# Attention and two feed-forwards: block products in the second feed-forward only, narrow buffers during attention

## The chip, the core and the metric

The kernel runs on one core of one Trainium2 chip. The core has a matrix engine (TensorE, PE in the profile), a vector engine (VectorE, DVE), a scalar engine (ScalarE, ACT), a general engine (GpSimd, POOL) and queues for transfers (DMA, here issued by SyncE, SP). Each engine works through its own instructions in the order in which the program lists them, and waits by semaphores for the others. The metric is the device time of one execution in microseconds; of several executions the median counts.

## What is computed

The reference is a local attention with summaries of blocks, and two feed-forwards behind it. Cut to what matters:

```python
# q, k, v: 2 x 8 x 768 x 64, fp32; moe_w_in 512 x 2048, moe_w_out 2048 x 512, both twice
k_sum, v_sum = blocks of 32 keys: max of k, mean of v
scores = softmax over (keys within 16 positions, 24 block summaries)
x = (scores @ [v, v_sum]) laid out as 1536 tokens x 512
h = x @ w_in;  x = (h * cos(h)) @ w_out            # first feed-forward
h = x @ w_in2; out = (h * clip(h + 3, 0, 6) / 6) @ w_out2   # second
```

All operands are fp32. The kernel keeps that accuracy with a pair for each number, a part in the type fp32r and the rest (`hi` and `lo`), and each product of two matrices becomes three on PE: hi with hi, lo with hi, hi with lo.

## The kernel before

**Stages.** Attention runs in 12 units of 128 tokens (`front(u)`: scores, largest, exponentials `es` with their sums, scaling by `rs` in line 610; `back(u)`: transposes to `pts` in line 625, the weighted sum in line 640, then `xhi` and `xlo`, the tokens for the feed-forwards). The 1536 tokens form three blocks of 512.

**Steps.** A feed-forward's 2048 hidden columns are 16 slices of 128. A step `s` of the list `plan` is one slice for one block: a first product `h` (`mm1`, line 780, twelve matmuls), a `middle`, and a second product (`mm2`, line 874, twelve matmuls) which adds into four banks of PSUM. The middle of the first feed-forward is five operations: a rounding on ACT (line 819), a difference on DVE (821), the sine on ACT (823), a product with `h` (825), then the pair of the result, `ghi` (389) and `glo` (834). Slices come in groups of four, each group for all three blocks in turn. The first 16 steps (`NEARLY`) are halves of 256 columns for blocks 0 and 1 and run during attention; steps 16 to 19 are block 2. Steps 20 to 55 are the rest of the first feed-forward, 56 to 103 the second.

**Sets.** From step `SETS` on (20), the first products of two neighbouring slices are made together (`mm1_set`, line 731): the 2 x 2 blocks of weights and tokens are combined so that seven block products of 256 columns do for eight, 7 x 3 x 2 = 42 matmuls instead of 24 of 512 columns. For that the weights of the two slices are combined and split into `phi` and `plo` (`convert_pair`, two such buffers), the tokens into `txhi` and `txlo` (`tees`; for the first feed-forward `first_tees`, line 705, which needs the sum of `xhi` and `xlo` first), and the products are joined into `hs` in SBUF by two copies (line 389) and five additions on DVE (line 744) per set. Before the sets, a slice's plain weights `whi` and `wlo` for the first product lie in the same memory as `phi` and `plo`, four slices of them.

**Weights.** Each 128 x 512 piece arrives as raw words (`raw`, 32 for each of the two sides, two buffers) and takes five operations to become fp32 values (`nearest`, lines 447 to 466) and two to become a pair (`split`, lines 389 and 406).

**Order.** Nothing stands in the order of the code. `Graph` collects all operations with what they read and write, and `forward` lists them for each engine: the operation that can start first goes first, and among those that can start about then the one with the earliest due time. An operation that may run on DVE or elsewhere is kept off DVE if the other engine would end no later than DVE plus `PATIENCE`; where DVE is still a choice, `UNWANTED` is added to its due time. An activation that needs another function table has `SWITCH` added. Where the planner leaves PE idle, `fill` puts matmuls with zeros into the order (lines 844 and 849), which keep PE working and change nothing. The second product of a step comes `LAG` = 2 steps behind its first.

**Memory.** `ch_c` (the middle's working buffer), `ghi` and `glo` are three buffers each of 512 columns, and a fourth pair once attention's memory is free. That is the operation `switch`: it gives attention's pool back and opens the pool `late`; what needs it reads the key `room`.

## Time and profile before

| | |
|---|---|
| device time, median of 3 runs | 615.45 us (614.9 to 615.78) |
| the profiled execution | 615.68 us |
| its span, first to last instruction | 614.0 us |
| PE busy | 592.5 us, 97% |
| DVE busy | 515.4 us, 84% |
| ACT busy | 389.2 us, 63% |
| POOL busy | 230.4 us, 38% |
| moved by DMA | 51.57 MB, 16 engines busy 25.2% of the span for it |
| granted PE clock, mean | 0.996 |

Times in the profile count from the first instruction. A matmul's row shows when it starts and for how long it is in the engine; as matmuls overlap, the distance between the starts of two of them is the time that one costs. L731 is line 731 of the kernel. `bank_c`, `bank_d` and so on are PSUM banks, their numbers left out.

### The profile page before, as it was taken

How to read it: one execution, taken by the hardware profiler on the slowest of the kernel's cores; microseconds unless marked ns; L12 is line 12 of the kernel's file. 1: busy time of each engine (PE TensorE's matmuls, PEld its weight loads, DVE VectorE, ACT ScalarE, POOL GpSimd, SP SyncE). 2: the span in 40 equal slices, each digit the busy share in tenths (PEclk: the TensorE clock that was granted, in tenths of full speed). 3: DMA queues.
4: the chain of work that ended last, by engine and by line, in shares of the span. 5: the costliest groups of instructions: out<-in, count | busy, mean ns of one | idle time of the engine just before them, and what ended most of it. 6: DMA issues, size and time to landing. Idle time of an engine off the chain costs nothing.

```text
span 614.0 us, 11095 instructions
## 1 busy us (share of the span) xinstructions
PE 592.5 (97%) x4244; PEld 519.5 (85%) x4244; DVE 515.4 (84%) x916; ACT 389.2 (63%) x828; POOL 230.4 (38%) x216
## 2 busy tenths in 40 slices
PE   9989899998998999999989999999999999999997
PEld 6678698887897888988978888999898989889895
DVE  4889997699999999899999999989869984984644
ACT  4889997675667667657776675685845643462321
POOL 5245531444232743473455554434334311520110
PEclk9999999999999999999999999999999999999999
DMA  8768631012112222111212012122312320200111
GB/s 275 226 233 254 183 122 52 2 69 69 34 36 69 69 69 69 70 68 70 76 62 70 25 46 69 49 90 98 108 69 70 114 92 1 70 1 1 69 70 68
DMA packets 17141, 51.57 MB, mean 84 GB/s; under 512 B 2112, under 2 KB 2112, under 8 KB 17088
## 3 DMA queue, kind: packets, MB, share of 16 engines
q1 hardware_dynamic: 17088, 50.86, 25.2%
q8 instruction: 33, 0.54, 0.4%
q14 instruction: 20, 0.16, 0.1%
HBM read 47.71 MB, written 3.15 MB: 83 GB/s over the span
## 4 chain that ended last, share of the span: by engine, by line
PE 55%; DVE 17%; ACT 6%; issue 3%; POOL 2%; DVEq 0%; ACTq 0%; POOLq 0%
PE bank_a L874 15%; PE bank_d L731 12%; PE bank_b L874 7%; PE bank_c L874 7%; PE bank_e L731 6%; PE bank_c L731 6%; DVE ch_c L821 2%; DVE hs L744 2%; DVE glo L834 1%; DVE ch_c L825 1%; DVE cv_t L464 1%; DVE ch_c L830 1%; ACT ch_c L823 1%; POOL cv_y L466 1%; ACT ch_c L819 1%
## 5 line engine op out<-in xcount | busy, mean ns | idle before, releaser
L466 POOL TENSOR_TENSOR cv_y<-cv_t,cv_y 128x512 int32<-128x512 int32 x29 | 42.4, 1463 | 75.9 <-DVE cv_t L464 64.8
L744 DVE TENSOR_TENSOR hs<-bank_d,hs 128x256 f32<-128x256 f32 x108 | 45.1, 421 | 29.3 <-PE bank_d L731 27.2
L834 POOL TENSOR_TENSOR glo<-ch_c,ghi 128x512 fp32r<-128x512 f32 (+1 forms) x28 | 34.2, 1227 | 52.5 <-ACT ghi L389 47.2
L389 ACT CAST ghi<-ch_c 128x512 fp32r<-128x512 f32 (+1 forms) x74 | 43.5, 592 | 11.6 <-DVE ch_c L825 5.4
L828 ACT ACTIVATE ch_c<-hs,three 128x512 f32<-128x512 f32 x48 | 33.7, 722 | 26.8 <-DVE hs L744 26.3
L464 DVE SCALAR_TENSOR_TENSOR cv_t<-raw,cv_t 128x512 int32<-128x512 int32 x64 | 49.2, 780 | 0.2
L457 ACT ACTIVATE cv_t<-raw 128x512 f32<-128x512 f32 x59 | 39.3, 670 | 6.2 <-DMA raw<-in_w_out_dram 2.3
L823 ACT ACTIVATE ch_c<-ch_c,half_pi 128x512 f32<-128x512 f32 (+1 forms) x56 | 35.8, 659 | 8.4 <-DVE ch_c L821 8.3
L830 DVE SCALAR_TENSOR_TENSOR ch_c<-ch_c,hs 128x512 f32<-128x512 f32 x48 | 36.9, 778 | 4.1 <-ACT ch_c L828 2.6
L447 ACT ACTIVATE cv_y<-raw 128x512 int32<-128x512 uint32 x54 | 35.8, 671 | 4.4 <-DVE wlj_out L406 3.5
L834 DVE TENSOR_TENSOR glo<-ch_c,ghi 128x512 fp32r<-128x512 f32 (+1 forms) x54 | 37.0, 692 | 1.7 <-POOL ghi L389 0.7
L731 PE MATMUL bank_d<-xhi,phi 128*128 128x256 f32 x170 | 34.7, 286 | 3.3 <-DVE hs L744 2.4
L731 PEld LDWEIGHTS bank_d<-xhi,phi 128*128 128x128 f32 x170 | 28.4, 189 | 8.3 <-DVE hs L744 3.9
L834 POOL TENSOR_TENSOR glj<-ch_c,ghj 128x512 fp32r<-128x512 f32 x11 | 15.9, 1443 | 51.5 <-ACT ghj L389 48.4
L462 DVE TENSOR_SCALAR cv_t<-cv_t 128x512 int32<-128x512 int32 x64 | 32.5, 516 | 2.3 <-ACT cv_t L457 2.2
L731 PE MATMUL bank_d<-xlo,phi 128*128 128x256 f32 x170 | 34.2, 283 | 0.0
L406 POOL TENSOR_TENSOR plo<-cv_y,phi 128x512 fp32r<-128x512 f32 (+1 forms) x16 | 18.6, 1161 | 41.6 <-DVE phi L389 33.8
L731 PE MATMUL bank_d<-xhi,plo 128*128 128x256 f32 x170 | 34.2, 282 | 0.0
L819 ACT ACTIVATE ch_c<-hs,quarter 128x512 int32<-128x512 f32 x36 | 24.9, 720 | 13.2 <-DVE hs L744 13.1
L821 DVE SCALAR_TENSOR_TENSOR ch_c<-hs,ch_c 128x512 f32<-128x512 f32 x36 | 31.2, 889 | 0.8 <-ACT ch_c L819 0.5
L825 POOL TENSOR_TENSOR ch_c<-hs,ch_c 128x512 f32<-128x512 f32 x14 | 20.7, 1486 | 29.5 <-ACT ch_c L823 29.5
L389 ACT COPY hs<-bank_d 128x256 f32<-128x256 f32 x39 | 14.5, 372 | 26.9 <-PE bank_d L731 26.5
(359 smaller groups left out, 2023.5 us busy)
## 6 DMA issues: line engine op xcount, KB each, us to landing
raw<-in_w_in_dram SPq DMA_DIRECT2D x32, 512.0 KB, 3.5
raw<-in_w_out_dram SPq DMA_DIRECT2D x32, 512.0 KB, 3.4
vcat<-in_vw_dram SPq DMA_DIRECT2D x12, 384.0 KB, 4.3
ktile<-in_kt_dram SPq DMA_DIRECT2D x8, 384.0 KB, 4.4
qt<-in_q_dram SPq DMA_DIRECT2D x12, 256.0 KB, 5.4
total<-in_vw_dram SPq DMA_DIRECT2D x16, 128.0 KB, 3.9
out_dram<-total SPq DMA_DIRECT2D x8, 256.0 KB, 2.0
vnat<-in_vw_dram SPq DMA_DIRECT2D x8, 128.0 KB, 5.8
```

Source lines behind the costliest of these rows:

```text
L389: nc.scalar.copy(o, i) if e == "ACT" else VEC[e].tensor_copy(o, i)
L447: nc.scalar.activation(y, low.bitcast(U32), AF.Copy, scale=2.0 ** -29)
L457: nc.scalar.activation(o, a, AF.Copy, scale=2.0 ** -112)
L464: G.op({"DVE": dve(DM)}, lambda e: nc.vector.scalar_tensor_tensor(t, high, -0x80000000, t, ALU.bitwise_and, ALU.bitwise_or), r=[rk], w=[tk ...
L466: G.op({"POOL": pool(DM), "DVE": dve(DM)}, lambda e: VEC[e].tensor_tensor(y, t, y, ALU.add), r=[tk], w=[yk], twice=True)
L731: nc.tensor.matmul(o, wt[i][:, A[a], kk * P:(kk + 1) * P], xt[:, kk, :], start=first and n + kk == 0, stop=n + kk == 3, skip_group_check=True)
L744: G.op({"DVE": dve(HALF)}, lambda e: nc.vector.tensor_tensor(o[0](), a, b[0](), ALU.add), r=[ak, b[1], "room"], w=[o[1]])
L821: G.op({"DVE": dve(N)}, lambda e: nc.vector.scalar_tensor_tensor(c(), h(), 0.5 / math.pi, c().bitcast(I32), ALU.mult, ALU.subtract), r=hk, ...
L823: G.op({"ACT": act(N) + 0.1}, lambda e: nc.scalar.activation(c(), c(), AF.Sin, bias=half_pi, scale=2.0 * math.pi), w=[ck], table="sin")
L830: G.op({"DVE": dve(N)}, lambda e: nc.vector.scalar_tensor_tensor(c(), c(), 6.0, h(), ALU.min, ALU.mult), r=hk, w=[ck], twice=bool(both))
L834: G.op({"DVE": dve(N), "POOL": pool(N)}, lambda e: VEC[e].tensor_tensor(glo[n][:, 0:N], c(), gh().bitcast(F32), ALU.subtract), r=[ck, gk], ...
L874: nc.tensor.matmul(acc(s, i)[0], l, r, start=first, stop=end and p == 2 and (N == TOK or i % 2 == 1), skip_group_check=N < TOK)
```

## The change

The change does five things.

1. Sets of seven block products are made in the second feed-forward only: `SETS` becomes 56. Steps 20 to 55 get plain first products of twelve 512-column matmuls, and `first_tees` goes. During the first feed-forward `phi` and `plo` hold the plain weights of six slices (`PER` = 3 in each of two buffers) instead of four; a slice's place is converted anew after its last use, and the first two pairs of the second feed-forward after the last use of the three slices that share the buffer.
2. During attention the working buffer and the result's pair have six buffers of 256 columns each (`ch_e`, `ghe`, `gle`), in attention's own pool, instead of three of 512.
3. Afterwards the first feed-forward has five working buffers, of which two are `hs`, and five pairs, of which one is a part of `txhi` and `txlo` that is not yet in use; which pair a step takes is settled ahead by `assign`. The second feed-forward has three and four.
4. Second products come three steps behind in the first feed-forward. All those of the 256-column steps are put ahead of `switch`.
5. The planner's numbers change: more patience with ACT and POOL, a higher price for DVE where there is a choice, a lower one for a change of table.

The diff, cut to its core (`ring_of` gives way to look-ups of the buffers, and the loop at the end first makes a list of events and then records them):

```diff
-LAG = 2
+LAG, LAG1 = 3, 3
...
-    PATIENCE = {"ACT": 0.3, "POOL": 0.3}
-    UNWANTED, SWITCH = 1.0, 8.0
+    PATIENCE = {"ACT": 0.6, "POOL": 0.6}
+    UNWANTED, SWITCH = 10.0, 3.0
...
-    NPLAIN = GROUPS[0][0]
-    SETS = NEARLY + NPLAIN
+    SETS = next(s for s in range(NSTEP) if plan[s][0])
...
-    NW0, NW1 = NPLAIN, 6
+    NW0, NW1 = 4, 6
     NPAIR = 2
+    PER = 3
...
-        t[f // per][:, f % per * 2:f % per * 2 + 2, :].rearrange("p a c -> p (a c)") for f in range(NPLAIN)]}
+        t[f // PER][:, f % PER * 2:f % PER * 2 + 2, :].rearrange("p a c -> p (a c)") for f in range(PER * NPAIR)]}
...
-    NC, NC1 = 3, 3
-    ch_c = ring(main, "ch_c", NC, [P, TOK])
-    NG, NG1 = LAG + 1, 4
-    ghi, glo = ring(main, "ghi", NG, [P, TOK], F32R), ring(main, "glo", NG, [P, TOK], F32R)
+    NC, NCL = 3, 5
+    NEC, NG1, NGL = 6, 4, 5
...
+    ch_e = ring(kv, "ch_e", NEC, [P, HALF])
+    ghe, gle = ring(kv, "ghe", NEC, [P, HALF], F32R), ring(kv, "gle", NEC, [P, HALF], F32R)
...
-            also = [(n, "in", f) for n in ("whi", "wlo") for f in range(NPLAIN) if f // per == i] if p < per + NPAIR else []
+            also = [(n, "in", PER * i + f) for n in ("whi", "wlo") for f in range(PER)] if p < NF // 2 + NPAIR else []
...
-    def first_tees(b):
...
+    gslot = {}
+
+    def assign():
+
+        free = list(range(NGL))
+        for what, s in events:
+            if s >= NEARLY and what == "second":
+                free.append(gslot[s])
+            elif s >= NEARLY and what == "middle":
+                gslot[s] = next(k for k in free if k < (NGL if s < SETS else NG1))
+                free.remove(gslot[s])
...
+    def attention_done():
+        every = [k for k in list(G.writer) if k[0] in (
+            "kt", "ks", "kcs", "kcw", "vn", "vcs", "vcw", "qt", "e", "mx", "sm", "rs", "pts", "ce", "ghe", "gle")]
+        every += ["vm", "b", "c0", "c1", "e"]
+        G.op({"NONE": 0.0}, switch, w=["room"] + every)
...
+        if s == NEARLY:
+
+            events += [("second", r) for r in pending] + [("switch", s)]
+            pending = []
+        if s < SETS:
+            events += [("first", s), ("middle", s)]
+        elif (s - SETS) % 2 == 0:
+            while len(pending) > 2:
+                events.append(("second", pending.pop(0)))
+            events += [("set", s), ("middle", s), ("middle", s + 1)]
+        events.append(("used", s))
+        pending.append(s)
+        lag = LAG if s < NEARLY else (LAG1 if s < SETS else 2)
+        while pending and pending[0] <= s - lag and (s < SETS or (s - SETS) % 2):
+            events.append(("second", pending.pop(0)))
...
+        elif s == uses[m, f]:
+            now = s
+            if n < NF - PER * NPAIR:
+                convert(n + PER * NPAIR, "in")
+            elif n < NF:
+
+                gone.add(n % (PER * NPAIR))
+                for i in range(NPAIR):
+                    if gone >= set(range(PER * i, PER * i + PER)):
+                        gone -= set(range(PER * i, PER * i + PER))
+                        convert_pair(NF // 2 + i)
+            elif n % 2:
+                convert_pair(n // 2 + NPAIR)
```

What this does to the order shows on PE and POOL. First PE, in the first feed-forward. Before, a set: `phi` and `plo` are the combined weights, `txhi` and `txlo` the combined tokens, and each row is two matmuls.

```order
L731 MATMUL bank_c_106<-xhi_96,phi_70 128x256 x2
L731 MATMUL bank_c_106<-xhi_96,plo_72 128x256 x2
L731 MATMUL bank_c_106<-xlo_99,phi_70 128x256 x2
L731 MATMUL bank_d_107<-txhi_1611,phi_70 128x256 x2
L731 MATMUL bank_d_107<-txhi_1611,plo_72 128x256 x2
L731 MATMUL bank_d_107<-txlo_1614,phi_70 128x256 x2
L731 MATMUL bank_d_108<-txhi_1611,phi_70 128x256 x2
L731 MATMUL bank_d_108<-txhi_1611,plo_72 128x256 x2
L731 MATMUL bank_d_108<-txlo_1614,phi_70 128x256 x2
L731 MATMUL bank_c_106<-xhi_96,phi_70 128x256 x2
L731 MATMUL bank_c_106<-xhi_96,plo_72 128x256 x2
```

The third bank is left after three products and the first is taken up again in the last row, while DVE and ACT read it out. Now, at the same stage, a plain first product stands among second products, here those of three steps earlier (`whj_out` is a slice's second weights):

```order
L775 MATMUL bank_d_98<-xhi_85,phi_69 128x512 x2
L775 MATMUL bank_d_98<-xhi_85,plo_71 128x512 x4
L775 MATMUL bank_d_98<-xlo_88,phi_69 128x512 x4
L893 MATMUL bank_a_93<-ghi_1711,whj_out_1702 128x512
L893 MATMUL bank_a_94<-ghi_1711,whj_out_1702 128x512
L893 MATMUL bank_b<-ghi_1711,whj_out_1702 128x512
L893 MATMUL bank_c_96<-ghi_1711,whj_out_1702 128x512
L893 MATMUL bank_a_93<-ghi_1711,wlj_out_1704 128x512
L893 MATMUL bank_a_94<-ghi_1711,wlj_out_1704 128x512
L893 MATMUL bank_b<-ghi_1711,wlj_out_1704 128x512
L893 MATMUL bank_c_96<-ghi_1711,wlj_out_1704 128x512
L775 MATMUL bank_d_99<-xhi_85,phi_70 128x512 x2
```

What moved: the seven short products with their reading out are gone, and each bank is written once by twelve long matmuls, then left alone for three steps.

Next POOL during attention, from the scaling of one unit's `es` to that of the next or nearly so. Before:

```order
L610 TENSOR_TENSOR es_123<-es_123,rs_136 128x960
L466 TENSOR_TENSOR cv_y_81<-cv_t_83,cv_y_81 128x512
L834 TENSOR_TENSOR glo_93<-ch_c_87,ghi_90 128x256
L834 TENSOR_TENSOR glo_91<-ch_c_85,ghi_88 128x256
L389 COPY kcat_116<-ktile_110 128x8x96
L834 TENSOR_TENSOR glo_92<-ch_c_86,ghi_89 128x256
L389 CAST ghi_90<-ch_c_87 128x256
L834 TENSOR_TENSOR glo_93<-ch_c_87,ghi_90 128x256
L389 CAST ghi_88<-ch_c_85 128x256
L834 TENSOR_TENSOR glo_91<-ch_c_85,ghi_88 128x256
L389 CAST ghi_89<-ch_c_86 128x256
L610 TENSOR_TENSOR es_124<-es_124,rs_136 128x960
```

Now (`cv_y` and `cv_t` are weights on their way to fp32, `ghe` and `gle` the narrow pair):

```order
L609 TENSOR_TENSOR es_132<-es_132,rs_145 128x960
L853 TENSOR_TENSOR gle_117<-ch_e_105,ghe_111 128x256
L388 CAST ghe_112<-ch_e_106 128x256
L853 TENSOR_TENSOR gle_118<-ch_e_106,ghe_112 128x256
L388 CAST ghe_107<-ch_e_101 128x256
L465 TENSOR_TENSOR cv_y_81<-cv_t_83,cv_y_81 128x512
L853 TENSOR_TENSOR gle_113<-ch_e_101,ghe_107 128x256
L388 CAST phi_70<-cv_y_81 128x512
L405 TENSOR_TENSOR plo_72<-cv_y_81,phi_70 128x512
L609 TENSOR_TENSOR es_133<-es_133,rs_144 128x960
```

What moved: in the old order the scalings between these two are on DVE; in the new one nearly all are on POOL, with casts and subtractions of weights and of the narrow pair between them. Over the whole attention POOL has ten of the twelve scalings instead of five, ACT has 15 changes of table up to the last exponential instead of 13, and the zero products between the first 256-column first product and the last weighted sum go from 15 of 512 and 24 of 256 columns to 13 and 18.

Last PE at the entry into the second feed-forward, now: the end of the second product of step 53, and the first set.

```order
L893 MATMUL bank_a_93<-glo_1714,whi_out_74 128x512
L893 MATMUL bank_a_94<-glo_1714,whi_out_74 128x512
L893 MATMUL bank_b<-glo_1714,whi_out_74 128x512
L893 MATMUL bank_c_96<-glo_1714,whi_out_74 128x512
L726 MATMUL bank_d_98<-xhi_87,phi_69 128x256 x2
L726 MATMUL bank_d_98<-xhi_87,plo_71 128x256 x2
L726 MATMUL bank_d_98<-xlo_90,phi_69 128x256 x2
L726 MATMUL bank_d_99<-txhi_1719,phi_69 128x256 x2
L726 MATMUL bank_d_99<-txhi_1719,plo_71 128x256 x2
```

Ahead of these rows stand the first product of step 55, whose last two matmuls come between second products, and the second products of 51 (its last quarter), 52 and 53. The set reads `phi_69` and `plo_71`, which held plain weights up to the first product of step 54.

## Rows read from the trace of the kernel before

**Rows 1.** the page, engines: busy us (share of the span) xinstructions.

```profile
PE 592.5 (97%) x4244; PEld 519.5 (85%) x4244; DVE 515.4 (84%) x916; ACT 389.2 (63%) x828; POOL 230.4 (38%) x216
```

**Rows 2.** stretch, us; PE, PEld, DVE, ACT, POOL busy (xinstructions); PE clock, DMA share, GB/s.

```profile
25.91:77.23 51.32, 47.19 (x556) 38.26 (x556) 47.24 (x93) 46.37 (x135) 24.90 (x23) 1.00 0.73 226
77.23:117.45 40.22, 38.64 (x511) 34.92 (x507) 29.67 (x62) 33.23 (x101) 9.06 (x12) 1.00 0.22 67
124.75:144.12 19.37, 19.37 (x96) 16.49 (x97) 18.51 (x31) 14.44 (x27) 6.12 (x6) 1.00 0.20 71
144.12:347.40 203.28, 195.40 (x1193) 173.82 (x1192) 190.17 (x322) 135.36 (x245) 92.50 (x67) 0.99 0.18 61
347.40:609.74 262.34, 260.37 (x1609) 233.21 (x1607) 208.01 (x375) 138.71 (x254) 81.61 (x64) 1.00 0.18 62
...
150.00:160.00 10.00, 9.34 (x47) 8.26 (x48) 9.96 (x20) 4.17 (x8) 1.51 (x1) 0.83 0.16 54
```

**Rows 3.** PE in time: start us, us, line, out<-in xcount [idle before <-releaser].

```profile
76.15 1.15 PE L640 MATMUL bank_e<-pts,vcat 120*64 120x64 f32 x32 [1.37 <-DVE vcat L389]
...
116.30 1.15 PE L640 MATMUL bank_e<-pts,vcat 120*64 120x64 f32 x32
```

**Rows 4.** PE in time: a plain first product; second products ahead of a set.

```profile
129.03 1.09 PE L780 MATMUL bank_d<-xhi,phi 128*128 128x512 f32 x4
...
131.78 0.28 PE L874 MATMUL bank_a<-ghi,whi_out 128*128 128x256 f32 x1
...
155.13 0.40 PE L874 MATMUL bank_b<-glo,whi_out 128*128 128x512 f32 x1
...
158.31 0.40 PE L731 MATMUL bank_c<-xhi,phi 128*128 128x256 f32 x2
158.55 0.40 PE L731 MATMUL bank_c<-xhi,plo 128*128 128x256 f32 x2
```

**Rows 5.** waits, 144.12 to 347.40: who waited for whom: us, times, longest.

```profile
PE bank_d L731 <- DVE hs L744: 4.3, 5, 1.9
...
PE bank_e L731 <- DVE hs L744: 2.2, 4, 1.0
```

**Rows 6.** PE in time: stops and zero products at the entry into the sets.

```profile
150.66 0.51 PE L731 MATMUL bank_d<-xhi,phi 128*128 128x256 f32 x2 [1.85 <-DVE hs L744]
...
161.91 0.40 PE L849 MATMUL bank_a<-zero 128*128 128x512 f32 x1
163.19 0.47 PE L731 MATMUL bank_d<-txhi,phi 128*128 128x256 f32 x2 [0.88 <-DVE hs L744]
...
163.97 0.62 PE L849 MATMUL bank_a<-zero 128*128 128x512 f32 x2
```

**Rows 7.** groups by line, 144.12 to 347.40: xcount | busy us, mean ns | idle before.

```profile
L821 DVE SCALAR_TENSOR_TENSOR ch_c<-hs,ch_c 128x512 f32<-128x512 f32 x36 | 31.2, 889 | 0.8 <-ACT ch_c L819 0.5
...
L744 DVE TENSOR_TENSOR hs<-bank_d,hs 128x256 f32<-128x256 f32 x48 | 20.0, 420 | 6.0 <-PE bank_d L731 5.0 <-ACT hs L389 0.3
```

**Rows 8.** groups by line, DVE, 124.75 to 144.12.

```profile
L821 DVE SCALAR_TENSOR_TENSOR ch_c<-bank_d,ch_c 128x512 f32<-128x512 f32 x2 | 1.4, 680 | 0.0
```

**Rows 9.** groups by line, 25.91 to 117.45.

```profile
L823 ACT ACT_TABLE_LOAD x7 | 9.0, 1283 | 0.1
...
L610 POOL TENSOR_TENSOR es<-es,rs 128x960 f32<-128x960 f32 x4 | 7.2, 1793 | 6.0 <-DVE rs L607 6.0
L610 DVE TENSOR_TENSOR es<-es,rs 128x960 f32<-128x960 f32 x6 | 6.9, 1156 | 0.2
...
L834 POOL TENSOR_TENSOR glo<-ch_c,ghi 128x256 fp32r<-128x256 f32 x7 | 5.1, 737 | 0.2
...
L406 POOL TENSOR_TENSOR plo<-cv_y,phi 128x512 fp32r<-128x512 f32 x2 | 2.6, 1284 | 7.7 <-DVE phi L389 4.5 <-ACT es L600 3.2
...
L389 POOL CAST ghi<-ch_c 128x256 fp32r<-128x256 f32 x5 | 2.0, 399 | 15.1 <-DVE ch_c L825 14.6 <-PE bank_d L780 0.5
```

**Rows 10.** PE in time, second feed-forward: its one stop.

```profile
379.03 0.74 PE L874 MATMUL bank_a<-whi_out,glo 128*128 128x512 f32 x2 [1.26 <-DVE glo L834]
```

More of the change, by code (lines that the diff above doesn't have):

```diff
@@ L866, in go @@
                 for p, i in group:
[L867 removed]
+                    l, r = parts[p][1]["out"][wi], gbuf(parts[p][3], s)[:, 0:N]
                     if m == 0:
@@ L994, in attention_two_ffn @@
+    events += [("second", r) for r in pending]
+    assign()
+    now = 0
+    for what, s in events:
         m, b, f, _, _ = plan[s]
         n = slices.index((m, f))
-        if s == SETS:
-            for c in dict.fromkeys(x[1] for x in plan[s:s + NPLAIN * NBLK]):
-                first_tees(c)
-        if s < SETS:
+        if what == "switch":
+            attention_done()
+            for k in range(NW0, NW1):
+                convert(k, "out")
+        elif what == "first":
+            now = s
```

102 lines of the change are left out of this document (50 added, 52 removed).

## The prediction

> **What bounds the kernel now.** I read the engines' shares first, then the same by stretches of the program, then TensorE (PE) in order of time at the borders of those stretches, and last what VectorE (DVE) does where PE stops. PE is busy 97% of the span and is the only engine close to it [rows 1]; the reader is to see that the rest of the argument is therefore an account of PE: its work at its pitch, and its stops.
>
> The stretches [rows 2] are: the two of attention (25.91, the first matmul of the first feed-forward, to 77.23, the end of the weighted sum of unit 6; from there to 117.45, the end of that of unit 11, the last [rows 3]); 7.3 us of leftovers; the four plain steps of block 2 (124.75 to 144.12); the 18 sets of seven products of the first feed-forward (144.12 to 347.40); and the second feed-forward with its 24 sets (347.40 to 609.74). The pitch of PE [rows 4]: twelve 512-column matmuls of a plain first product take 131.78 - 129.03 = 2.75 us, two 256-column ones of a set 0.24, so a set of 42 takes 42 x 0.12 = 5.04; and fourteen of the second product start in 158.31 - 155.13 = 3.18, 0.227 each, so a second product of twelve takes 2.73.
>
> With these the stretch 124.75 to 347.40 (222.65 us) holds 4 x 2.75 + 18 x 5.04 + 38 x 2.73 + 2 x 1.44 (two leftover second products of 256 columns, 12 x 0.12) = 11.0 + 90.7 + 103.7 + 2.9 = 208.3 us of work. 14.3 us are not work. The four plain steps have none of it (PE busy 19.37 of 19.37); all of it lies among the 18 sets, where DVE is busy 190.17 of 203.28 us [rows 2]. Where PE stops there, the releaser is the addition of product sums on DVE: 4.3 and 2.2 us of waits of PE for line 744 [rows 5]. One stop costs more than itself: after the 1.85 us ahead of 150.66 [rows 6] the granted clock of 150 to 160 is 0.83 [rows 2], a stretch partly at the lower of the two levels (1.2 and 2.4 GHz), and the 12 + 20 matmuls from there to 158.31 take 7.65 us for 1.44 + 4.54 at full pitch: 1.7 us lost.
>
> The second feed-forward is different: 24 x 5.04 + 50 x 2.73 = 257.5 of 262.34, with DVE at 208.01.
>
> **The change part by part.**
>
> *Plain products in the first feed-forward.* 18 sets (756 matmuls of 256 columns) become 36 plain steps (432 of 512). At the entry of the second feed-forward both orders have issued the second products up to the same one (slice 53), so the stretch compares directly: after, 40 x 2.75 + 38 x 2.73 = 213.7 us. Before it took 222.65, less the 2.9 of the two leftovers, which now lie ahead of it (below): 219.8. The work alone gives -6.1: the sets save 36 x 2.75 - 18 x 5.04 = 8.3 us of PE and cost 14.3.
>
> Whether the plain steps stop PE too: the nearest row, the four plain ones, says 0; the farthest, the stretch of the sets, 203.28 - 195.40 = 7.9 of idle time. I take 1.0, near the plain row, since DVE gets lighter: 90 additions of 0.420 go (37.8 us), and 36 products with the first operand drop from 889 ns, with `hs` read from SBUF, to 680, with a bank read [rows 7, 8], 7.5 us. The 14 of line 825 that ran on GpSimd (POOL) must run on DVE, which alone can read the bank: 14 x 0.68 = 9.5 back. 190 - 45 + 10 = 155 us of DVE in some 215, instead of 190 in 203. The order also leaves room: a second product now stands behind three later first products, some 16 us after its own, so a chain of five operations of 0.7 us has time. **-5.1 us.**
>
> The Trainium skill ("TensorE: Matmul & The Clock Gate", "Back-to-back issue gap") gives isolated warm gaps of N / 2.4 ns + 2.5, 109 ns for 256 columns and 216 for 512. By that the sets would save 10.6 us, not 8.3, and the time would be an estimated 2.3 us longer than mine. The trace has 120 and 227 to 229 [rows 4], and the measurement decides.
>
> *Six buffers of 256 columns, three slices behind, other patience.* In the order of before 37 zero products stand between the first feed-forward's first matmul and unit 11, 15 of 512 and 22 of 256 columns, and 2 later ones before 117.45; now 13 and 18, none after unit 6. Two of 0.23 and six of 0.12 are 1.2 us. At the last weighted sum PE has one more first product behind it (fifteen instead of fourteen) and half a second product more: the work that leaves the next stretch. From 77.23 PE idles only 40.22 - 38.64 = 1.6 us, so this work is gained only if idle time ahead goes: PE idles 51.32 - 47.19 = 4.1 us in the first stretch of attention, and its zero products are 15 x 0.23 + 22 x 0.12 = 6.1 [rows 2]. DVE loses five of seven scalings of `es` up to the last, 5 x 1.156 = 5.8 us; POOL gains five of 1.793 = 9.0 [rows 9]. ScalarE (ACT) loads two more tables, 2 x 1.283 = 2.6 us, hidden while ACT idles (40.22 - 33.23 = 7.0 from 77.23); uncovered, they cost 2.6. Bounds: -10 (all idle time and zero products of 25.91 to 77.23: 4.1 + 6.1) and +9.6 (second rival). I take what the order shows, **-1.2**.
>
> The weight transfers are the same 64 on the same queue. Two more `w_in` slices are converted during attention, two fewer afterwards; their steps lie on DVE, ACT and POOL beside the above.
>
> *Entry into the second feed-forward.* `phi` and `plo` now hold plain weights until the last steps of the first. The pair for the first set can be written only after the first product of slice 54, the next after that of 55. PE has the first product of 55 and three second products in front of the set: 2.75 + 3 x 2.73 = 10.9 us, for four casts and four subtractions, of which the longest, a subtraction on POOL, takes 1.28 [rows 9]: about 5 us if the two kinds overlap. What waits in the queues behind a late pair is the casts and subtractions of the following slices on ACT, POOL and DVE, and PE behind them. Bounds: -1.3 (the one stop of the second feed-forward, ahead of 379.03, vanishes [rows 10]) and +5.1 (the entry into sets of the kernel before: 1.85 and 0.88 of stop, 1.7 of low clock and three zero products, 0.7 [rows 6]). I take **+1.0**, nearer the low end: in the kernel before, a pair regularly has one set with its second products, 10.5 us, for the same work.
>
> The tees of the first three blocks go with the sets: 48 operations on DVE, POOL and ACT, beside PE. The end is untouched.
>
> Sum: 614.0 - 5.1 - 1.2 + 1.0 = 608.7 of span. The profiled execution took 615.68, 1.68 more than its span, and stands 0.23 above the median 615.45: 608.7 + 1.68 - 0.23 = **610.1 us**.
>
> **The rivals.**
>
> *The entry stops PE as the old entry did*: +5.1 instead of +1.0, 614.2. For it: the first set's weights come free late and in one go. Against: 10.9 us of cover.
>
> *Attention is paced by POOL, slower.* Place: POOL's queue between two scalings. In the order shown, the eight operations between the scalings of two units sum to 2 x 1.28 + 3 x 0.74 + 2 x 0.40 = 5.6 us and a cast of 512 columns that has no row here, with the scaling 7.4 and that cast [rows 9]; units 7 to 11 come every 8 us (116.30 - 76.15 = 40.15 for five [rows 3]). If five scalings each come later by 1.793 - 1.156 = 0.64 and by one operation of 1.28, the last unit is 9.6 us late, and PE, which has no zero product left there, stops: 610.1 + 1.2 + 9.6 = 620.9. It decides once POOL's load passes one unit's 8 us. Against it: POOL is busy 9.06 of the last 40.22 us and two units are in flight. The Trainium skill ("GPSIMD Engine Reference", "8. Key points") states that POOL shares SBUF interfaces with DVE, which contend where a DVE instruction has two SBUF inputs. The trace agrees in kind (889 against 680 ns), and by it more POOL work would slow both.
>
> *Attention gets much shorter*, because DVE paced it: half of the 10.2 us of idle time and zero products goes, 5.1 instead of 1.2: 606.2. For it: DVE is busy 47.24 of 51.32 there. Against: ACT, with 46.37, gets more to do.
>
> *The change does not do what it says*: the 14.3 us come from weights or banks, not from the additions, and stay: 610.1 - 1.0 + 14.3 = 623.4. Against: the plain steps, with the same weights, had none.
>
> **How the numbers follow.** Forecast 0.62 (its own range 606.5 to 613.2), late entry 0.12, POOL 0.12, shorter attention 0.12, no effect 0.02. A measurement of this kernel tells about 0.2% from no change, 1.2 us: faster is below 614.2, slower above 616.7. Faster: 0.62 less 0.02 for its tail, half of the 0.12 of the late entry, and 0.12: 0.78. Within: 0.06 + 0.02 = 0.08. Slower: 0.12 + 0.02 = 0.14. The range leaves out the two slow cases (0.14) and the lower part of the short attention (0.05): 605.5 to 616.0.
>
> **What would show it.** Right: from the last weighted sum to the first set PE without stops of over 0.5 us, plain steps every 5.5 us, DVE below 80% there, no low clock; the second feed-forward some 262 to 264 us long; the first 512-column first product about 2 us later than 124.75, as 2.9 us of work moved ahead of it and 1.2 were saved. Wrong: PE waiting for `es` or `pts` in attention with POOL busy; a stop at the first or second set with a cast or subtraction of `phi` or `plo` as releaser; or stops between plain steps that DVE does not explain.

## The result, and the profile after

The changed kernel takes 607.88 us (median of 4 runs, 605.82 to 608.47), the kernel before 615.17 beside it on the same chip: a ratio of 0.9876, 95% interval 0.985 to 0.9902. It is faster by 7.3 us; 5.3 were forecast (610.1), and the time lies inside the range. The profiled execution took 608.47 with a span of 606.8.

The engines' shares, as [rows 1] of before (engine, busy us, share of the span, instructions):

```profile
PE 592.8 (98%) x3908; PEld 506.7 (84%) x3908; DVE 444.8 (73%) x743; ACT 362.0 (60%) x750; POOL 226.1 (37%) x247
```

PE works for the same 592 us in a span that is 7.2 us shorter, with 71 us less of DVE. The stretches, as [rows 2]; columns: stretch, its length, then busy us of PE, PEld, DVE, ACT and POOL with their instructions, granted PE clock, DMA share, GB/s.

```profile
26.93:77.23 50.30, 45.91 (x572) 36.60 (x572) 44.17 (x82) 46.10 (x134) 31.98 (x30) 1.00 0.69 224
77.23:117.45 40.22, 39.97 (x487) 36.70 (x488) 32.84 (x66) 37.58 (x106) 26.98 (x30) 1.00 0.34 105
125.68:138.62 12.94, 12.94 (x59) 10.70 (x58) 9.48 (x15) 11.33 (x21) 5.77 (x6) 1.00 0.23 81
138.62:337.87 199.25, 199.25 (x881) 164.98 (x880) 135.48 (x208) 109.50 (x174) 52.36 (x50) 1.00 0.18 59
337.87:602.89 265.02, 260.87 (x1609) 232.72 (x1607) 205.09 (x343) 136.68 (x249) 96.97 (x89) 1.00 0.18 62
```

From 125.68, the first 512-column first product, to 337.87, the first set, PE never stops (199.25 of 199.25, 12.94 of 12.94), where before 7.9 us of idle time lay among the sets; DVE is busy 135.48 of 199.25 us, 68% instead of 94%. PE's order in time at two places (start, duration, line, out<-in, count):

```profile
125.68 1.09 PE L775 MATMUL bank_d<-xhi,phi 128*128 128x512 f32 x4
...
149.28 0.61 PE L775 MATMUL bank_e<-xhi,phi 128*128 128x512 f32 x2
...
154.72 0.61 PE L775 MATMUL bank_c<-xhi,phi 128*128 128x512 f32 x2
```

A plain step takes 154.72 - 149.28 = 5.44 us, twelve matmuls of a first and twelve of a second product at 0.227 each. Against the prediction's terms, on the two profiled executions:

| term | forecast | measured |
|---|---|---|
| up to the first 512-column first product (124.75 + 2.88 of work moved ahead = 127.63 before; now 125.68) | -1.2 | -1.95 |
| from there to the first set (219.8 before; now 337.87 - 125.68 = 212.19) | -5.1 | -7.6 |
| second feed-forward (262.34 before; now 265.02) | +1.0 | +2.7 |
| after the last second product (4.26 before; now 606.8 - 602.89 = 3.91) | 0 | -0.35 |
| sum of the span | -5.3 | -7.2 |

The first row depends on the execution. Six kernels of this document (the changed one and, of those below, the two with added load on DVE, the one with a lag of two in the plain steps, the one with shifted places and the one without the tokens' arithmetic) have the same order on all engines up to the first 512-column product, and it starts at 123.12 to 125.68 us in them; the changed kernel's profile is the latest. Their first matmul of the first feed-forward comes at 25.92 to 26.95, and most of what else differs is one wait of PE for `pts` near 33 us, from nothing to 2.23 us (1.70 in the changed kernel's profile, 1.53 in that of before).

The two longest stops that are left late in the program are at the entry into the second feed-forward (the bracket is idle time and its releaser):

```profile
344.15 0.51 PE L726 MATMUL bank_d<-xhi,phi 128*128 128x256 f32 x2 [1.15 <-DVE hs L739]
...
357.44 0.50 PE L726 MATMUL bank_d<-txhi,plo 128*128 128x256 f32 x2 [1.24 <-DVE plo L405]
```

### The profile page after: what moved, and what is told of

Same layout as the page of the kernel before. It is cut to its first block, busy times and chain, and to the rows that moved or that the text cites. A ratio compares the mean times of both kernels' runs of the same rounds, so it can differ in the third digit from the quotient of the medians.

```text
span 606.8 us, 10193 instructions
## 1 busy us (share of the span) xinstructions
PE 592.8 (98%) x3908; PEld 506.7 (84%) x3908; DVE 444.8 (73%) x743; ACT 362.0 (60%) x750; POOL 226.1 (37%) x247
## 4 chain that ended last, share of the span: by engine, by line
PE 77%; DVE 12%; ACT 7%; issue 1%; DMA 1%; POOL 1%; ACTq 0%; POOLq 0%
PE bank_a L893 19%; PE bank_d L775 11%; PE bank_b L893 8%; PE bank_c L893 8%; PE bank_d L726 8%; PE bank_e L775 4%; PE bank_c L775 4%; PE bank_e L726 4%; PE bank_c L726 4%; ACT es L599 2%; DVE glo L853 2%; DVE ch_c L849 1%; DVE cv_t L463 1%; PE bank_e L516 1%; DVE cv_t L461 1%
## 5 line engine op out<-in xcount | busy, mean ns | idle before, releaser
L853 DVE TENSOR_TENSOR glo<-ch_c,ghi 128x512 fp32r<-128x512 f32 x55 | 44.2, 815 | 6.9 <-ACT ghi L388 5.5
L388 ACT CAST ghi<-ch_c 128x512 fp32r<-128x512 f32 x62 | 38.1, 620 | 17.8 <-DVE ch_c L849 9.5
L456 ACT ACTIVATE cv_t<-raw 128x512 f32<-128x512 f32 x59 | 39.6, 673 | 10.9 <-DMA raw<-in_w_in_dram 3.9
L739 DVE TENSOR_TENSOR hs<-bank_d,hs 128x256 f32<-128x256 f32 x60 | 25.3, 422 | 23.5 <-PE bank_d L726 22.3
L775 PE MATMUL bank_d<-xhi,phi 128*128 128x512 f32 (+1 forms) x144 | 35.7, 348 | 0.2 <-ACT phi L388 0.2
L775 PE MATMUL bank_d<-xhi,plo 128*128 128x512 f32 (+1 forms) x144 | 32.8, 347 | 0.7 <-POOL plo L405 0.7
L775 PE MATMUL bank_d<-xlo,phi 128*128 128x512 f32 (+1 forms) x144 | 32.1, 343 | 0.0
L599 ACT ACTIVATE es<-bank_c,nmx 128x120 f32<-128x120 f32 x88 | 30.4, 375 | 0.6 <-DVE nmx L591 0.5
L465 DVE CUSTOM_DVE_ANT_0 cv_y<-cv_t,cv_y 128x1024 uint16<-128x1024 uint16 x39 | 29.7, 774 | 1.2 <-ACT cv_y L446 0.4
L775 PEld LDWEIGHTS bank_d<-xhi,plo 128*128 128x128 f32 x144 | 23.8, 189 | 4.6 <-POOL plo L405 1.1
L775 PEld LDWEIGHTS bank_d<-xlo,phi 128*128 128x128 f32 x144 | 23.9, 189 | 3.1
```

Of the source, the lines that this page charges most:

```text
L388: nc.scalar.copy(o, i) if e == "ACT" else VEC[e].tensor_copy(o, i)
L456: nc.scalar.activation(o, a, AF.Copy, scale=2.0 ** -112)
L465: G.op({"POOL": pool(DM), "DVE": dve(DM)}, lambda e: VEC[e].tensor_tensor(y, t, y, ALU.add), r=[tk], w=[yk], twice=True)
L599: nc.scalar.activation(ef[:, c, :], s4[j][:, hp, :], AF.Exp, bias=nmx[:, c:c + 1], scale=scale, accum_out=sm[:, c:c + 1])
L775: nc.tensor.matmul(h, w["in"][i][:, kk * P:(kk + 1) * P], x[blk][:, kk, c0:c1], start=p + kk == 0, stop=p == 2 and kk == NK - 1)
L853: G.op({"DVE": dve(N), "POOL": pool(N)}, lambda e: VEC[e].tensor_tensor(gbuf("lo", s)[:, 0:N], c(), gh().bitcast(F32), ALU.subtract), r=[* ...
```

## The experiments

Three questions were open. Why do plain products not stop PE: because DVE has less to do, or because a plain product does not depend on DVE in time? What part have the buffers and the planner's numbers? And what made the entry into the second feed-forward dearer than forecast? L numbers in the fences are those of each kernel's own code; line 726 (before 731) is always the set, 739 (before 744) its addition into `hs`.

### What stopped PE in the first feed-forward

**The plain products alone.** Three of the five parts are taken back:

```diff
-LAG, LAG1 = 3, 3
+LAG, LAG1 = 2, 2
-    PATIENCE = {"ACT": 0.6, "POOL": 0.6}
-    UNWANTED, SWITCH = 10.0, 3.0
+    PATIENCE = {"ACT": 0.3, "POOL": 0.3}
+    UNWANTED, SWITCH = 1.0, 8.0
-    NEC, NG1, NGL = 6, 4, 5
+    NEC, NG1, NGL = 3, 4, 5
```

> The changed kernel with three of its five parts taken back: second products two slices behind in both stages, three narrow buffers during attention instead of six, and the planner's old patience and switch costs. What is left is the plain first products of steps 20 to 55 with their five working buffers. Theory 1 (the gain comes from the plain products, because the sets' additions filled VectorE and stopped TensorE): the stretch from the first 512-column first product to the first set is within 2 us of the changed kernel's 212.2, the time 608 to 611. Rival (the gain comes from the order: lag, buffers, patience): 613 to 617, with stops of TensorE between the plain steps.

Measured: 612.82 us, ratio 0.9962 (0.995 to 0.9974), between the two expectations. The stretch from the first 512-column product to the first set is 213.64 us (127.01 to 340.65), within 2 us of 212.2, as theory 1 said. The stops are gone without the other parts: from the last weighted sum to the first set PE is busy all the time.

```profile
117.89:340.65 222.76, 222.76 (x1031) 186.16 (x1028) 158.74 (x249) 126.25 (x204) 48.28 (x39) 1.00 0.17 57
340.65:607.03 266.38, 261.17 (x1609) 233.05 (x1607) 208.79 (x379) 137.36 (x249) 71.64 (x55) 1.00 0.18 61
```

The rest of the gain is not there: the work up to the first 512-column product is shorter by only 0.6 us (127.01 against 127.63), and the second feed-forward takes 266.38, 4.0 us more than before.

**The planner's numbers alone**, on the kernel before:

```diff
-    PATIENCE = {"ACT": 0.3, "POOL": 0.3}
-    UNWANTED, SWITCH = 1.0, 8.0
+    PATIENCE = {"ACT": 0.6, "POOL": 0.6}
+    UNWANTED, SWITCH = 10.0, 3.0
```

> The kernel before with only the planner's new numbers (patience 0.6, unwanted 10, switch 3). Theory 1: the sets of the first feed-forward keep some 14 us that are not work, and the time stays at 613 to 618. Rival (the order makes the gain): 608 to 611, VectorE well below 190 us in the sets of the first feed-forward.

Measured: 636.53 us, ratio 1.0347 (1.0325 to 1.0368), outside both expectations: slower by 21 us. All of it lies beside sets: the first 512-column product stands at 124.58 us (124.75 before), the 18 sets of the first feed-forward take 216.18 us (143.85 to 360.03) instead of 203.28, and the second feed-forward 271.88 instead of 262.34. The stretch from 140 us on, then the second feed-forward, and the longest waits of PE in the first of the two (who waited for whom: us in all, times, longest):

```profile
140.00:360.03 220.03, 208.75 (x1227) 182.47 (x1226) 192.43 (x298) 135.78 (x243) 121.18 (x95) 0.98 0.17 58
360.03:631.91 271.88, 263.20 (x1618) 234.90 (x1616) 210.30 (x356) 140.47 (x256) 95.02 (x88) 1.00 0.17 60
```

```profile
PE bank_d L731 <- ACT hs L389: 4.3, 3, 3.1
PE bank_a L874 <- ACT ghj L389: 2.0, 1, 2.0
PE bank_d L731 <- DVE hs L744: 1.6, 3, 0.8
```

In the 18 sets DVE has 293 instructions instead of 322, but is busy for 188.57 us, nearly the 190.17 of before; its share is 87% instead of 94% because the stretch is longer. PE is idle for 11.3 us there, and the granted clock is 0.98. Of 10.9 us of waits 6.5 are for a late reader of a bank, now ACT's copy of the sums into `hs` as well as DVE's addition; 3.3 are for results of the middle and 1.1 for weights. So a full DVE is not the only thing that makes a reader late. Whether it is the load or the date that stops PE, this run does not tell.

**The kernel before with less on DVE.** The product with `h` is left out in the steps of the first feed-forward's sets:

```diff
-            G.op({"DVE": dve(N), **both}, lambda e: VEC[e].tensor_tensor(c(), h(), c(), ALU.mult),
-                 r=hk, w=[ck], twice=bool(both))
+            if s < SETS:
+                G.op({"DVE": dve(N), **both}, lambda e: VEC[e].tensor_tensor(c(), h(), c(), ALU.mult),
+                     r=hk, w=[ck], twice=bool(both))
```

> The kernel before without the product with h (line 825) in the 36 steps of the first feed-forward that are made in sets: that part of the computation is left out, TensorE's work is the same. 22 of these products lay on VectorE and 14 on GpSimd. Theory 1 (load of VectorE as such): VectorE falls from 190 to some 170 us of its stretch, the 14.3 us that are not work fall below 7, the time to 606 to 610. Rival (the short way inside a set: a product's bank must be added into SBUF before the bank's next product, whatever the load): the stops ahead of sets with line 744 as releaser stay, 613 to 616.

Measured: 612.32 us, ratio 0.9954 (0.9941 to 0.9968). It does not separate the theories, because it did not do enough: the planner filled DVE again, from 144 to the second feed-forward it is busy 182.49 of 197.37 us, 92%. PE's idle time there fell from about 8 to 4.8 us, and the stop of 1.83 us ahead of 150.34 stayed. The second feed-forward, where nothing was changed, took 264.27 us instead of 262.34: a different order alone moves it by that much.

**The changed kernel with more on DVE.**

```diff
+        for j in range(1 + s % 2 if NEARLY <= s < SETS else 0):
+            G.op({"DVE": dve(N)}, lambda e, j=j: nc.vector.tensor_tensor(
+                hs[2 + j], c(), gh().bitcast(F32), ALU.subtract),
+                r=[*ck, gk, "room"], w=[("h", 2 + j, 0), ("h", 2 + j, 1)], twice=True)
```

> The changed kernel with VectorE loaded as it was before: in steps 16 to 55 the last subtraction of the middle (ghi and glo) is made once or twice more, into hs, which nothing reads there: 1.5 more operations of 512 columns a step, some 50 us, 135 to about 185 of 199 us. Theory 1 (load as such): TensorE stops between plain steps, by 5 to 14 us in all, and the time is 613 to 622. Rival (it is the short way inside a set): the plain steps, whose banks have four steps' time, take the load without stops over 0.5 us; under 610.

Measured: 606.23 us, ratio 0.9861 (0.9841 to 0.9881), no slower than the changed kernel. The plain steps from 138 us on:

```profile
138.00:336.23 198.23, 198.23 (x876) 164.13 (x875) 172.88 (x253) 108.88 (x176) 66.95 (x55) 1.00 0.18 59
```

DVE is busy 172.88 of 198.23 us, 87%, the share that it had beside the first feed-forward's sets in the kernel with the new numbers alone, where PE was idle for 11.3 us; here PE does not stop once. My own theory, that the additions filled DVE and so stopped PE, falls as it stood: beside plain steps this load costs nothing. The 94% of before was not reached.

**The same load beside sets.**

```diff
+        for j in range(2 if s >= SETS else 0):
+            G.op({"DVE": dve(HALF)}, lambda e, j=j: nc.vector.tensor_tensor(
+                spare[0], c()[:, j * HALF:(j + 1) * HALF], gh()[:, j * HALF:(j + 1) * HALF].bitcast(F32), ALU.subtract),
+                r=[*ck, gk, "room"], w=["spare"], twice=True)
```

> The changed kernel with the added load of e7 in the second feed-forward instead of the first, that is, beside sets instead of plain steps: in steps 56 to 103 the last subtraction of the middle is made once more, in two operations of 256 columns into a spare buffer that nothing reads; 96 operations, some 46 us, 205 to about 250 of 265 us of VectorE. Theory 3 (formed after e7: neither the load nor the sets stop TensorE alone; a set's copies and additions have a date, the next product of their bank, and other work queued ahead of them on VectorE makes them miss it): stops with the addition into hs (line 739) as releaser come back, 5 to 15 us more in the second feed-forward, 270 to 280 instead of 265, time 612 to 622. Rival (the sets of the first feed-forward stopped for something of their own, the product with the sine, the tables, the tokens): the load is taken here as in e7, second feed-forward at 264 to 266, time 606 to 609.

Measured: 619.07 us, ratio 1.0073 (1.0053 to 1.0093), as theory 3 said. The second feed-forward takes 276.70 instead of 265.02, with 11.5 us of idle time instead of 4.2; 8.4 us of its waits are for line 740, the addition into `hs` (2.6 in the changed kernel), and none is for a working buffer or a result that the added operations hold longer:

```profile
335.64:612.34 276.70, 265.22 (x1614) 233.70 (x1612) 245.51 (x426) 136.64 (x253) 120.72 (x98) 1.00 0.18 59
```

```profile
PE bank_c L727 <- DVE hs L740: 4.2, 3, 1.8
PE bank_d L727 <- DVE hs L740: 3.8, 5, 1.2
```

The longest stop, on PE and on DVE (each row: start, duration, line, out<-in, count, idle time before and releaser):

```profile
454.88 0.40 PE L727 MATMUL bank_e<-xlo,phi 128*128 128x256 f32 x2
457.11 0.50 PE L727 MATMUL bank_c<-txhi,phi 128*128 128x256 f32 x2 [1.84 <-DVE hs L740]
```

```profile
453.00 1.51 DVE L857 TENSOR_TENSOR spare<-ch_c,ghi 128x256 f32<-128x256 f32 x1
454.44 0.68 DVE L854 TENSOR_TENSOR glo<-ch_c,ghi 128x512 fp32r<-128x512 f32 x1
455.04 0.41 DVE L857 TENSOR_TENSOR spare<-ch_c,ghi 128x256 f32<-128x256 f32 x1
455.38 0.41 DVE L461 TENSOR_SCALAR cv_t<-cv_t 128x512 int32<-128x512 int32 x1
455.71 0.41 DVE L857 TENSOR_TENSOR spare<-ch_c,ghi 128x256 f32<-128x256 f32 x1
456.05 0.68 DVE L463 SCALAR_TENSOR_TENSOR cv_t<-raw,cv_t 128x512 int32<-128x512 int32 x1
456.65 0.41 DVE L740 TENSOR_TENSOR hs<-bank_c,hs 128x256 f32<-128x256 f32 x1
```

The product before in this bank ended at about 454, and PE wants the bank again at 455.3 (457.11 less 1.84), two other products later; the addition that empties it is 0.41 us long, but stands behind three added subtractions (line 857), one of the kernel's own and two conversions of weights in DVE's list, and starts at 456.65. So the four corners are there: plain steps with DVE at 68% and at 87% stop PE for 0.00 us; sets stop it for 4.2 us at 77% (205.09 of 265.02) and 11.5 at 89%. The corners are not quite alike, since the middles of the two feed-forwards differ and the added load is 37 us of DVE in one and 40 in the other; the sets of the first feed-forward at 87%, with their 11.3 us, agree. Neither the load nor the sets do it alone. A set's copies and additions have a date, since the bank is wanted again two products later, and what stands ahead of them in the list decides whether they keep it.

### Lag, buffers, numbers

Each of three parts of the changed kernel is taken back by itself. Two slices behind in the plain steps instead of three:

```diff
-LAG, LAG1 = 3, 3
+LAG, LAG1 = 3, 2
```

> The changed kernel with second products two slices behind in the plain steps of the first feed-forward, instead of three. My account said that the third slice gives the middle's chain of five operations its time. If that matters: stops of TensorE between plain steps with the chain's last operation as releaser, 609.5 to 614. If two slices (some 10 us) are enough for the chain: no stops, 607.5 to 608.5.

Measured: 608.48 us, ratio 0.99 (0.9885 to 0.9915), the same within the measurement. No stop between the plain steps: two slices, some 11 us, are enough for the chain of the middle.

The old numbers of the planner:

```diff
-    PATIENCE = {"ACT": 0.6, "POOL": 0.6}
-    UNWANTED, SWITCH = 10.0, 3.0
+    PATIENCE = {"ACT": 0.3, "POOL": 0.3}
+    UNWANTED, SWITCH = 1.0, 8.0
```

> The changed kernel with the planner's old patience, unwanted and switch costs alone. If these numbers made the 1.95 us that were gained up to the first 512-column first product: 609 to 610.5, and that product later than 125.7. If the six buffers and the lag made it: within 0.7 us of the changed kernel's 607.9.

Three narrow buffers and two slices behind in attention:

```diff
-LAG, LAG1 = 3, 3
+LAG, LAG1 = 2, 3
-    NEC, NG1, NGL = 6, 4, 5
+    NEC, NG1, NGL = 3, 4, 5
```

> The changed kernel with three narrow buffers and second products two slices behind during attention, all else as changed. If the deeper buffers bring the early gain: the first 512-column first product, with its work ahead of it the same, about 2 us later, 609 to 611. If they bring nothing: within 0.7 us of 607.9.

Measured: 612.33 us (ratio 0.9962, 0.9948 to 0.9976) with the old numbers, more than expected, and 613.24 (0.9976, 0.9964 to 0.9987) with three buffers, more again. From the first matmul of the first feed-forward to the first set all of these kernels have the same work, so their difference is idle time, zero products and low clock. The changed kernel, old numbers, three buffers, and both with the shorter lag (the plain products alone), in this order, from four profiles:

```profile
26.93:337.87 310.94, 306.30 (x2073) 257.15 (x2073) 224.37 (x374) 208.48 (x440) 118.57 (x117) 1.00 0.28 91
```

```profile
26.67:341.98 315.31, 309.42 (x2076) 258.90 (x2077) 244.42 (x430) 205.91 (x430) 81.12 (x76) 0.99 0.28 89
```

```profile
26.71:342.69 315.98, 309.22 (x2084) 258.96 (x2083) 228.82 (x379) 210.47 (x443) 118.30 (x112) 1.00 0.28 89
```

```profile
26.20:340.65 314.45, 311.08 (x2108) 261.89 (x2109) 237.07 (x408) 208.77 (x443) 86.82 (x77) 1.00 0.28 89
```

The zero products in this stretch are 13 of 512 columns and 18 of 256 in the changed kernel, 16 and 20, 22 and 20, and 15 and 52 in the others. At 0.227 and 0.12 us they are 5.1, 6.0, 7.4 and 9.6 us. Idle time is 4.6, 5.9, 6.8 and 3.4. With the old numbers a part of the time from 26 to 46 us also runs at the lower clock (granted 0.88 and 0.95 in its halves, some 1.7 us). Taken back alone, each of the two parts costs 4 to 5 us of this stretch; with neither it costs 3.5. An execution of the changed kernel's order may differ by some 2 us there (309.2 to 311.5 in the six kernels named with the result), which leaves all three well apart from it. They gain only together. That six buffers need POOL's help in attention, and the reverse, would fit, but no run shows how. That was not in my account, which named no price for either.

### The entry into the second feed-forward

DVE's list in the changed kernel ahead of the stop at 344.15:

```profile
340.19 1.28 DVE L463 SCALAR_TENSOR_TENSOR cv_t<-raw,cv_t 128x512 int32<-128x512 int32 x1
341.38 1.78 DVE L853 TENSOR_TENSOR txlo<-ch_c,txhi 128x512 fp32r<-128x512 f32 x1
343.08 0.68 DVE L465 CUSTOM_DVE_ANT_0 cv_y<-cv_t,cv_y 128x1024 uint16<-128x1024 uint16 x1
343.69 0.41 DVE L739 TENSOR_TENSOR hs<-bank_d,hs 128x256 f32<-128x256 f32 x1
```

The bank that PE wants again at 343.0 (344.15 less 1.15) is full at about 341.6, and its addition starts at 343.69, behind a subtraction of 1.78 us and a conversion. It is the same mechanism as above, at the place where the pairs of weights, the tees and the last closings all come due. Two of the rows, 1.28 and 1.78 us, are also longer than the same operations while POOL does nothing (in this kernel 0.68 for line 463, mean of 49, and 0.69 for such a subtraction, see the last section). By an estimate from these figures the addition would otherwise come 1.7 us earlier, which is more than the stop. Two experiments took away from the queue. First the weights' places are shifted by two, so that the first buffer of pairs is free after step 52 instead of 54:

```diff
-        i = slot(*slices[n]) if side == "out" else n % (PER * NPAIR)
+        i = slot(*slices[n]) if side == "out" else (n + 2) % (PER * NPAIR)
...
-        i = slot(m, f)
+        i = (f + 2) % (PER * NPAIR)
...
-                gone.add(n % (PER * NPAIR))
+                gone.add((n + 2) % (PER * NPAIR))
```

> The changed kernel with the plain weights of the first feed-forward in places shifted by two, so that the first of the two buffers for pairs is free after step 52 and not 54; the second is free after step 55 as before. Theory A (the two stops at the entry into the second feed-forward, 1.15 and 1.24 us, come from weights and sums that all fall due at once on VectorE): with the first pair converted some 11 us earlier the backlog is spread, both stops shrink, and the second feed-forward, 265.0 us, is 262.5 to 263.5; time 605.5 to 606.5. Rival (the second pair alone is late, and the backlog comes from the tokens): the second feed-forward stays at 264.5 to 265.5, time 607.5 to 608.5.

Then the tokens' arithmetic is left out as well (the lines with `sub(...)` and the addition in `tees`, twelve operations):

> The kernel of e9 (places shifted by two) without the twelve additions and subtractions of the tokens' blocks at the entry into the second feed-forward (lines 680 and 698, 512 columns each): that part of the computation is left out, the splits into parts and TensorE's work stay. If the tokens' arithmetic, some 11 us of VectorE and GpSimd between 300 and 370, is what the remaining stops of the first five sets wait behind: these stops (0.28, 0.81, 0.28 in e9) go, the second feed-forward is 261.5 to 262.5 instead of 263.5. If it is the weights' own way: it stays at 263 to 264.

Measured: 606.14 us (ratio 0.9861, 0.9844 to 0.9877) and 602.26 (0.9799, 0.9776 to 0.9821). The second feed-forward, first with the places alone, then without the tokens' arithmetic:

```profile
336.51:599.97 263.46, 260.23 (x1609) 232.94 (x1607) 200.58 (x332) 135.23 (x245) 99.76 (x90) 1.00 0.17 58
```

```profile
335.30:596.74 261.44, 259.50 (x1609) 233.00 (x1607) 191.10 (x326) 132.72 (x241) 94.64 (x89) 1.00 0.17 58
```

With the places shifted, time and stretch came out as theory A said. Without the tokens' arithmetic the stretch fell as the first expectation said, just below its 261.5 to 262.5. Of the 2.7 us more than before, 1.6 went with the earlier pair, and another 2.0 without the tokens' arithmetic. That does not make the arithmetic the cause by itself, since the kernel before has it too and takes 262.34: less in the queue, of either kind, lets the additions come in time. Nor is the 1.6 exact. Where the order is the same the stretch repeats (265.02, and 265.05 in the kernel with three narrow buffers), but over the six kernels with the late pair and no load added there, most of them in an order of their own, it is 264.37 to 266.38.

What stays in the second kernel is a stop of 0.71 us near 360 and two of 0.61, near 458 and 522; the kernel before had 0.23 at the places of the last two.

That pointed to the numbers, which keep work off DVE beside sets too. The last kernel has the shifted places, and the new numbers up to 118 us of the planner's clock only:

```diff
+        OLD = 118.0
...
-                    other = min(start(i, e, at) + c - self.PATIENCE[e] for e, c in engines.items() if e != "DVE")
+                    early = start(i, "DVE", at) < OLD
+                    other = min(start(i, e, at) + c - (0.6 if early else 0.3) for e, c in engines.items() if e != "DVE")
```

and `UNWANTED` and `SWITCH` in the same way.

> The kernel of e9 with the planner's new patience, unwanted and switch costs up to 118 us of its own clock only, the end of attention, and the old ones from there. If the new numbers are worth something in attention alone and cost a little beside sets, as e2 (264.5 in the second feed-forward with a late pair) against the changed kernel (265.0) points to: second feed-forward 262 to 263, time 604.5 to 606. If they cost nothing there: as e9, 605.5 to 606.8. If GpSimd's help is needed at the entry into the sets: second feed-forward 264 to 266, 607 to 609.

Measured: 605.3 us (603.53 to 606.87), ratio 0.9834 (0.9814 to 0.9854). The second feed-forward takes 262.64, as expected of a small cost beside sets:

```profile
337.82:600.46 262.64, 260.74 (x1609) 233.15 (x1607) 201.95 (x365) 134.00 (x245) 72.97 (x58) 1.00 0.16 58
```

Apart from the one without the tokens' arithmetic, this is the fastest kernel by its median, 2.6 us below the changed one; the intervals of the two ratios still touch (0.9814 to 0.9854, and 0.985 to 0.9902), so the row above, 2.4 us shorter, is the better evidence. Against the shift of the places alone (606.14) the time decides nothing, and the stretch, 262.64 against 263.46, is one execution of each. What the numbers cost beside sets can be seen at the two stops. First with the new numbers there (places alone; PE, DVE, POOL), then with the old (the last kernel; PE, DVE):

```profile
461.16 0.50 PE L726 MATMUL bank_e<-xhi,phi 128*128 128x256 f32 x2 [0.61 <-DVE hs L739]
458.99 1.78 DVE L853 TENSOR_TENSOR glo<-ch_c,ghi 128x512 fp32r<-128x512 f32 x1
460.69 0.41 DVE L739 TENSOR_TENSOR hs<-bank_e,hs 128x256 f32<-128x256 f32 x1
458.62 1.60 POOL L465 TENSOR_TENSOR cv_y<-cv_t,cv_y 128x512 int32<-128x512 int32 x1 [2.17 <-DVE cv_t L463]
```

```profile
459.55 0.51 PE L728 MATMUL bank_e<-txhi,phi 128*128 128x256 f32 x2 [0.23 <-DVE hs L741]
458.48 0.67 DVE L855 TENSOR_TENSOR glo<-ch_c,ghi 128x512 fp32r<-128x512 f32 x1
459.08 0.41 DVE L741 TENSOR_TENSOR hs<-bank_e,hs 128x256 f32<-128x256 f32 x1
```

With the new numbers POOL converts weights beside the subtraction ahead of the addition, and the subtraction takes 1.78 us instead of 0.67. So it is at both places in all seven kernels that have the new numbers there and no load added beside sets, with stops of 0.60 or 0.61 us; in the five with the old numbers the subtraction takes 0.67 or 0.68 and the stops are 0.23 or 0.24. That is 0.75 us, and as the changed kernel has it too (at 464.09 and 528.32), this part of its 2.7 does not belong to the entry.

## Why the prediction was right, and where its steps failed

**PE as the bound, and the account by stretches**: right. The same 592 us of PE, and the 7.2 us are found by adding four stretches. That the sum came within 2 us is in part luck: three stretches gained 3.6 us more than forecast, and the second feed-forward lost 1.7 more.

**The work of the plain steps**: right, with a small error of the pitch. I took 2.75 us for a first product, read between two rows whose border costs a little; 78 products of twelve take 212.19 us, 2.72 each. That is 1.5 us of the 2.5 by which the term was too small. The measured work that sets had saved is 36 x 2.72 - 18 x 5.04 = 7.2 us, not 8.3. By the Trainium skill ("TensorE: Matmul & The Clock Gate", "Back-to-back issue gap"), whose formula is for isolated matmuls, it would have been an estimated 10.6; the trace, with 120 and 227 ns from start to start, does not agree.

**Stops among the plain steps**: 1.0 taken, 0.00 measured; the other 1.0 us of that term. The reason that I gave was half wrong. I wrote that DVE gets lighter, and that the third slice gives the chain time. With DVE as full as in the first sets of another kernel (87%) there is still no stop, and with two slices there is none. What removes the stops is that nothing of a plain product has to be done on DVE before a date that lies two products ahead. The prediction had the right rows for this, the releaser in [rows 5] and the bank taken up again in the order, and put the share of DVE beside them as the cause.

**Narrow buffers, lag, patience**: -1.2 forecast, -1.95 measured. The zero products lost 1.2 us as read from the order (15 and 24 to 13 and 18), PE's idle time up to the border went from 6.0 to 4.6, and the first matmul came 1.0 us later (26.93 against 25.91; over the kernels here it is 25.91 to 27.16, and within one order it differs by as much, so this does not come from the change). Counted from that matmul the gain is 3.0 us (98.75 against 98.84 + 2.88): the term was less than half of it, and a late start of the profiled execution hid 1.0 of it. The zero products and the idle time make 2.5 of the 3.0; the remaining 0.5 is not located. What failed besides is the split that I did not make: the two parts gain only together, and the numbers alone, which I had counted as a detail of attention, bring nothing there on the kernel before and cost 21 us beside its sets.

**Entry**: +1.0 forecast, +2.7 measured, of which 0.75 are the two later stops of the new numbers; the term was too small. The step that failed is the cover of "10.9 us, for four casts and four subtractions": it counted the pair's own operations and not the list that they and the sets' additions stand in. From 337.87 to 370 DVE is busy 30.71 of 32.13 us in the changed kernel. I had put the tees among the things that "go with the sets"; those of the second feed-forward are still there, now beside a late pair, and without their arithmetic 2.0 us go.

**The rivals.** The entry as the old one (+5.1) came in part, by a different way: not the weights alone, also the tokens. POOL as the pace of attention did not come: PE waits once for a scaling of `es`, for 0.5 us, and its 2.2 us for `pts` (1.8 before) are for ACT.

```profile
PE bank_b L624 <- ACT pts L388: 2.2, 2, 1.7
PE bank_b L624 <- POOL es L609: 0.5, 1, 0.5
```

The much shorter attention did not come. That the stops stay came out wrong: there are none.

**What would show it**: plain steps every 5.44 us (5.5), no stop from the last weighted sum to the first set, DVE at 68%, clock 1.00: right. The first 512-column product came 0.9 us later than before, not about 2, and the second feed-forward at 265.02 lies above 262 to 264. A stop at the second set with a subtraction of `plo` as releaser, named among what would be wrong, is there (357.44).

## What to carry to other kernels

Where a trick saves matmuls by more reading out of PSUM, its price is not the busy time of the reading engine but the date of each reading: look at what stands ahead of the reading in that engine's list. Nearly the same load added 0 us of stops beside products that leave their bank alone for several steps, and over 7 us beside products that take it up again two products later. A planner's weights tuned for one stage should be tried on each stage alone: here the same numbers gain in attention, though only with the six buffers, and cost 0.8 us beside the sets of one kernel and 21 in another.

## What the runs showed of the hardware

A subtraction of 512 columns with two inputs in SBUF takes DVE 0.69 us when POOL does nothing: in the changed kernel, behind 130 us, 77 such operations (lines 405 and 853) have a mean of 0.687 and none is over 0.695. Where POOL works for at least 0.3 us of their time, 29 have a mean of 1.175 and the longest is 1.78. The 1.78 us at 341.38 above is one; POOL does this beside it:

```profile
339.62 1.29 POOL L693 TENSOR_TENSOR txlo<-total,txhi 128x512 fp32r<-128x512 f32 x1 [3.90 <-ACT txhi L388]
340.88 1.73 POOL L405 TENSOR_TENSOR plo<-cv_y,phi 128x512 fp32r<-128x512 f32 x1
```

The Trainium skill ("Trainium Architecture — The Big Picture", "What this means for kernel authors") says that the pair of ports which DVE and POOL share is locked by one of them at a time, not divided. The rows agree: POOL's subtraction ends at 342.6, and the one on DVE that had begun at 341.38 ends at 343.16, 0.55 us later, as if it had worked only from about then on. For this kernel it means that work given to POOL is not free for DVE's dates, and the two stops of 0.6 us that the new numbers bring beside sets, with a subtraction of 1.78 us ahead of the addition, are a case of it. How much of the entry's stops it makes was not measured by itself.
